# Forget-gate attention and a bilinear feed-forward layer: the two loads of f on two queues, and a new order of all operations

## The chip, the core and the metric

One NeuronCore of one Trainium2 chip. Five engines work beside each other, each through its own list of instructions in order: TensorE (PE; its weight loads are shown as PEld), VectorE (DVE), ScalarE (ACT), GpSimd (POOL) and SyncE (SP), which here only issues DMA transfers. An engine waits on semaphores for the work of others. Matrix products go to PSUM, of which the kernel uses eight banks: four single ones ("ff") and two pairs ("sc"). The metric is the time of one execution on the device in microseconds (us).

## What is computed

Attention with a forget gate over 8 batches of 8 heads, 576 positions of 64 channels, then a feed-forward layer without activation over the 4608 tokens of 512 channels:

```python
scores = scale * np.matmul(q, k.transpose(0, 1, 3, 2))
cum = np.cumsum(np.log(np.clip(f, 0.0001, 1.0)), axis=-1)
decay = cum[:, :, :, None] - cum[:, :, None, :]
scores = np.where(causal, -1000000000.0, scores + decay)
attn = softmax(scores)                       # max taken off, sum + 1e-9
x = (attn @ v).transpose(0, 2, 1, 3).reshape(B * S, H * D)
out = (x @ w_a) * (x @ w_b) @ w_out          # 512 -> 1536 -> 512
```

## The kernel before

The kernel first makes a list of 2353 operations (class `Op`): each has an engine (or a choice of engines), a planned duration, what it depends on, which buffers it takes, and a function that issues its instructions. Then it issues them in an order that is written out in the file as numbers (`ORDER`, at the end), with one letter for each operation that has a choice of engine (`CHOICE`: D, A, P for DVE, ACT, POOL, S for SP), and with the buffer that each taker of a ring gets (`SLOTS`). `laid_out` (L1330) reads the two lists. The order is not one in time: it fixes the list of every engine, and semaphores do the rest.

**Attention** runs in 32 units t = 4 b + pair, each of a batch b and a pair of heads. The 576 queries of a unit are five blocks of rows: 0 to 3 with 128 rows each, 4 with the last 64 rows of both heads. Per unit: PE makes the scores (`sc`, operations qk), DVE takes the maximum of each row (in batch 0) or adds the decay and takes the maximum in one instruction (L674, later batches), ACT exponentiates with the sum (L705; result in PA for blocks 0 to 2 and PB for 3 and 4), DVE inverts the sums (L715), and the probabilities are normalised (`do_norm`, L717: operations norm, mostly on POOL, L726). They are transposed, by PE in batch 0 and partly in batch 1 (`pe_tr`, L742, `psP`: operations ptr, and pev for the copy out of PSUM), else by a DMA transpose on SP's queue (`do_tr`, L736, operations tr, results PTA and PTB). PE multiplies them with v (`do_pv`, L755, pv; pvx for a whole unit), and a copy puts the result into xT (ev). "norm3.0" is a normalisation of unit 3, block 0; there are two, one for each head.

**Loads.** q and k of batch 0 are loaded by POOL's queue with conversion. From batch 1 on SP loads a half batch of q or k at a time as float32 (576 KB, L339), and POOL scales or casts it (`cast_qk`, operations ca1q0 and so on, L291 and L293); PE transposes it into qT or kT (pt, `psT`). The float32 buffers are a ring of three. v of batches 0 and 1 is loaded by POOL (lds, L305), weights too (ldwa, ldwb, ldwo, L510); POOL is then occupied with issuing.

**f** (8 x 8 x 576 values) goes into one tile of the S ring, two halves on partitions 0 to 31 and 64 to 95 (`f_load`, L211, issued at L213). DVE clips it (L225), ACT takes the logarithm (L260), DVE runs the prefix sum (`scan`, L228), all of it in two pieces of columns, 0 to 255 and 256 to 575. A 16-bit high part (L264) and low part (`low_part`, L233, four operations) go into crow, from which PE adds the decay to the scores of batch 0. SP stores the sums to DRAM (`cum_store`, L238), and later units load them spread over all partitions.

**Feed-forward.** xT is cut into groups of 256, 256, 256, 384, six times 512, and 384 tokens. For every group PE makes x w_a (psa) and x w_b (psb), each in groups of matmuls into one PSUM bank (`ff_mm`), ACT copies psa (acopy, L289), DVE multiplies it with psb (mul, L1073), PE multiplies with w_out (pso) and ACT or DVE copies the result for the store. The first psa needs the rows 0 to 255 of all four units of batch 0: blocks 0 and 1, that is norm, ptr, pev, pv and ev of units 0 to 3. Every product is issued as two halves of 64 output partitions (`mm_halves`, L74), which run side by side.

Before that PE has too little to do; 24 operations `wake` (L79, four matmuls on the identity each) stand between its other work.

Of the kernel before, what the change touches and what calls it, by code (L numbers as in the profile page):

```python
# [25 lines left out]
def kernel(  # L26
# [78 lines left out]
    def paddings():  # L105
# [36 lines left out]
        PA:03212103210321032103210321032103;PB:01010101010101010101010101010101;S:010110010110100110101010100101  # L142
        00101010101011101010101011010100111011011001001011010111010101010101011100001010101010;a16:0210210210210
        21021021021021012012012012012012102101201201201201201210212101201012012010210210121010210210210210210;bc
        :0210210210210210210210210210;ff:03120313021332010331032103231232320013100203120103212130213021021032031
        20312031202120131102310230210312031023102310230123123102132013201201320123103213012312301231213201321023
        01321020132013203120312013201321321302103210321032132132013023120320310132103210321032131203121023102130
        23023203103130213213201320132103210312012312031231030123021021021301302130123013013211302012012013202301
        230210231023120312301321302301023021021021021023120121023013203203203203201;ht:0dcba981234567d0bc9a18325
        4760dbc9a187352460da9bc13786524d0a931bc578624d019a35bc7286d9401ab35c728496db01a5c73248906;n16:0101001010  # L150
        10101101010101010010;n32:0210212010210102012012012102101201210120202102;nv:01010101;osb:0101010100101010
        00101101010011010101;qd:010101010101010101010101;sc:0101010101010101101010101010010101010000011010010101
        0100110101101010110101010100010110101001011010101001010100110101010010101010;st:054321054320154320154320
        15432015
# [86 lines left out]
    o_f = [Op(None, {"SP": 0.5, "ACT": 0.5}, lambda e, half=half: f_load(e, half), prio=-310, land=0.3, name=f"ldf{half}") for half in range(2)]  # L241
# [967 lines left out]
    for n in cuts:  # L1209
# [3 lines left out]
        0 1 52 46 29 30 2 62 5 3 53 47 58 4 31-33 37 38 34 39 35 40 42 41 43 267 279 262 6 7 48 54 8 9  # L1213
# [3 lines left out]
        66 141 339 340 21-23 264 67 220 226 94 179 76 96 232 133 221 227-229 271 222 231 180 233 234 84  # L1217
# [4 lines left out]
        200 163 196 1710 292 281 293 1712 201 295 309 310 302 296 303 283 297 1713 164 1715 1714 311-313  # L1222
# [17 lines left out]
        567 698 520 560 534 533 559 540 615 659 630 624 623 625 631 1791 1792 633 632 1790 440-442 569  # L1240
        704 626 491 576 705 492 598 627 599 583 706 619 1793-1798 707 653 714 600 601 1799 614 493 586
# [4 lines left out]
        655 592 564 671 1823 606 721 726 657 664 730 737 738 1824 683 678 732 731 1825 1826 739-741 1827  # L1246
# [3 lines left out]
        811 649 753 1849 776 1850 608 1851 1852 748 750 777 1853-1855 727 901 1857 781 754 788 783 782  # L1250
# [9 lines left out]
        1903 886 880 935 948 942 949 918 919 930 1904 1905 888 950 889 1906-1908 953 1910 1909 1912 809  # L1260
        1013 1101 936 1911 954 1914 891 890 1913 920 810 1915 955 972 929 970 887 881 975 867 927 1019
        882 976 937 922 875 978 1916 1920 1918 990 983 1917 985 1921 892 984 977 991 993 893 894 1919
        956 974 1922 1925 992 979 986 958-960 1923 943 997 980 994 1107 961 998 962 973 1108 1109 1926
# [110 lines left out]
```

## Time and profile before

| | us |
|---|---|
| median of three runs | 402.25 |
| these runs | 400.26, 402.25, 405.24 |
| the profiled execution | 400.81 |
| its span, first to last instruction | 399.0 |
| start of the first psa, from the span's start | 40.70 |
| ACT busy | 288.1 |
| DVE busy | 295.6 |
| POOL busy | 259.1 |

The granted clock of PE has a mean of 0.996 over the span. All times of the profile count from the span's start. A line of the timeline gives start, duration, engine, source line, operation, output and inputs with their shapes, how many instructions are merged, and in brackets how long the engine stood idle before and what ended that. A line of the chain of waits gives start, duration and what the end of the program waited for at that moment; "issue" is time without a wait that the profile shows.

### The profile page before, as it was taken

The page shows a single profiled execution, that of the slowest core. Times are in us where ns is not written, and L with a number is a line of the kernel's source. Part 1 is how long each engine was busy: PE and PEld are TensorE (multiplying, and loading weights), DVE is VectorE, ACT ScalarE, POOL GpSimd, SP SyncE. Part 2 cuts the span into 40 slices and gives each one's busy share as a digit, 9 for nine tenths or more (in the row PEclk, how much of TensorE's full clock was granted, in tenths as well). Part 3 has the DMA queues.
Part 4 walks back from the last instruction along what each step waited for, and adds up shares of the span by engine and source line. Part 5 has one row for each costly group of instructions (what it writes and reads, how often), then busy time and mean ns, then how long its engine had stood idle before and what let it go on. Part 6 is the DMA issues. An engine that isn't in the chain of part 4 may idle for free.

```text
span 399.0 us, 14669 instructions
## 1 busy us (share of the span) xinstructions
PE 388.0 (97%) x5768; PEld 241.0 (60%) x5768; DVE 295.6 (74%) x973; ACT 288.1 (72%) x799; POOL 259.1 (65%) x468
## 2 busy tenths in 40 slices
PE   6988999999999999999999999999999999999997
PEld 3545886978857655555555655555555556555675
DVE  6866899999989979886978887889888780243241
ACT  4996998899889887878887887867887772332131
POOL 8398866698798789596879789687847871000000
PEclk9998999999999999999999999999999999999999
DMA  8899999999999999999999999999997677200102
GB/s 125 232 199 150 128 146 169 285 187 290 248 261 254 246 250 246 226 279 275 266 200 277 258 246 208 254 260 324 183 173 201 113 125 143 86 2 27 54 28 81
DMA packets 147365, 76.87 MB, mean 193 GB/s; under 512 B 124384, under 2 KB 128352, under 8 KB 147296
## 3 DMA queue, kind: packets, MB, share of 16 engines
q1 hardware_dynamic: 132816, 68.65, 75.3%
q0 software_dynamic: 14256, 7.08, 14.6%
q8 instruction: 45, 0.74, 0.7%
q10 hardware_dynamic: 224, 0.21, 0.2%
q14 instruction: 24, 0.20, 0.1%
HBM read 52.05 MB, written 9.58 MB: 154 GB/s over the span
## 4 chain that ended last, share of the span: by engine, by line
PE 88%; DMA 4%; POOL 3%; issue 1%; DVE 1%; ACT 1%; SPq 1%; ACTq 0%; POOLq 0%; DVEq 0%
PE psb L74 23%; PE psa L74 23%; PE pso L74 23%; PE sc L551 4%; PE pvx L769 3%; PE sc L539 2%; PE psT L359 2%; PE psP L74 2%; DMA q<-in_q_dram 2%; PE sc L74 2%; DMA PTA<-PA 2%; POOL PA L726 1%; PE pv L769 1%; PE pvx L784 1%; DMA cum_f<-in_f_dram 1%
## 5 line engine op out<-in xcount | busy, mean ns | idle before, releaser
L674 DVE CUSTOM_DVE_ANT_0 S<-sc,spread 64x576 f32<-64x576 f32 (+4 forms) x232 | 125.2, 561 | 9.9 <-ACT PA L705 2.8
L74 PE MATMUL psa<-xT,wa 128*64 128x512 f16 (+2 forms) x1056 | 113.1, 341 | 0.1
L74 PE MATMUL psb<-xT,wb 128*64 128x512 f16 (+2 forms) x1056 | 113.0, 341 | 0.0
L1073 DVE TENSOR_TENSOR ht<-psb,a 128x512 f16<-128x512 f32 (+1 forms) x114 | 74.1, 659 | 39.3 <-PE psb L74 29.4
L74 PE MATMUL pso<-wout,ht 128*64 128x512 f16 x840 | 101.7, 380 | 0.0
L289 ACT CAST a<-psa 128x512 f16<-128x512 f32 (+1 forms) x114 | 63.2, 557 | 53.1 <-PE psa L74 45.6
L726 POOL TENSOR_SCALAR PA<-PA,st 128x256 f16<-128x256 f16 (+2 forms) x182 | 85.8, 484 | 12.7 <-DVE st L715 11.5
L705 ACT ACTIVATE PA<-S,st 128x256 f16<-128x256 f32 (+2 forms) x168 | 84.1, 503 | 8.2 <-DVE st L674 8.1
L726 POOL TENSOR_SCALAR PB<-PB,st 128x512 f16<-128x512 f16 (+1 forms) x91 | 64.2, 713 | 24.6 <-DVE st L713 11.3
L74 PEld LDWEIGHTS <-wa 128*64 128x64 f16 x1056 | 57.8, 110 | 34.1 <-issue 3.4
L74 PEld LDWEIGHTS <-wb 128*64 128x64 f16 x1056 | 57.6, 110 | 31.5 <-issue 1.3
L74 PEld LDWEIGHTS <-ht 128*64 128x64 f16 x912 | 48.0, 110 | 34.5 <-issue 0.9
L705 ACT ACTIVATE PB<-S,st 128x512 f16<-128x512 f32 x56 | 40.2, 719 | 4.5 <-DVE st L674 4.3
L705 ACT ACTIVATION_READ_ACCUMULATOR PA<-S,st 128x1 f32 x168 | 32.0, 190 | 0.0
L293 DVE COPY osb<-pso 128x512 f32<-128x512 f32 x18 | 12.4, 688 | 19.7 <-DMA out_dram<-osb 10.1
L631 POOL TENSOR_SCALAR_AFFINE_SELECT spread<-spread 128x768 f32<-128x768 f32 x24 | 20.9, 872 | 7.7 <-DMA spread<-cum_d 7.6
L769 PEld LDWEIGHTS <-nv 128*64 128x64 f16 x640 | 21.7, 110 | 6.6 <-DMA PTA<-PA 0.8
L701 ACT ACTIVATE PB<-S,st 128x576 f16<-128x576 f32 x28 | 21.7, 774 | 4.6 <-POOL spread L631 1.2
L674 DVE CUSTOM_DVE_ANT_1 S<-sc,spread 128x256 f32<-128x256 f32 x48 | 19.5, 419 | 6.1 <-ACT xT L289 1.9
L674 DVE DVE_READ_ACCUMULATOR2_ANT st<- 128x1 f32 (+1 forms) x280 | 23.0, 82 | 0.0
L715 DVE RECIPROCAL st<-st 128x2 f32<-128x2 f32 x128 | 18.2, 156 | 6.3 <-ACT PB L705 3.7
L551 PE MATMUL sc<-kT,qT 64*128 64x512 f16 (+4 forms) x144 | 21.3, 333 | 0.8 <-ACT PA L705 0.4
(106 smaller groups left out, 490.3 us busy)
## 6 DMA issues: line engine op xcount, KB each, us to landing
spread<-cum_d SPq DMA_DIRECT2D x24, 576.0 KB, 6.2
out_dram<-osb SPq DMA_DIRECT2D x35, 256.0 KB, 3.1
q<-in_q_dram SPq DMA_DIRECT2D x14, 576.0 KB, 5.6
k<-in_k_dram SPq DMA_DIRECT2D x14, 576.0 KB, 5.4
v<-in_v_dram SPq DMA_DIRECT2D x24, 256.0 KB, 5.9
wout<-in_moe_w_out_dram POOLq DMA_DIRECT2D x3, 512.0 KB, 5.8
nv<-in_v_dram POOLq DMA_DIRECT2D x8, 128.0 KB, 4.2
wa<-in_moe_w_a_dram POOLq DMA_DIRECT2D x2, 512.0 KB, 6.5
```

Of the source, the lines that this page charges most:

```text
L74: nc.tensor.matmul(out=out[r], lhsT=lhsT[:, r], rhs=rhs, **kw)
L289: nc.scalar.copy(out=out_, in_=in_)
L293: VEC[e].tensor_copy(out=out_, in_=in_)
L551: nc.tensor.matmul(out=dst, lhsT=lhsT, rhs=rhs, start=start, stop=stop, skip_group_check=True)
L631: nc.gpsimd.affine_select(out=c[:, :, 0:SM].rearrange("p h (j k) -> p h j k", k=128), in_=c[:, :, SM:2 * SM].rearrange("p h (j k) -> p h j ...
L674: nc.vector.tensor_tensor_reduce(out=o, in0=x, in1=y, scale=-1.0, scalar=3e38, op0=ADD, op1=MIN, accum_out=m)
L701: nc.scalar.activation(out=p_blocks(t, 4), in_=T[("s" if direct else "z", t, 4)], func=EXP, bias=st[:, 8:9], scale=sign, accum_out=st[:, 1 ...
L705: nc.scalar.activation(out=p_blocks(t, i)[:, :, h, :], in_=(T[("s", t, i)][:, h, :] if direct else T[("z", t, i)][:, h * n:h * n + n]).rea ...
L715: nc.vector.reciprocal(out=st[:, 20 + 2 * i:22 + 2 * i], in_=st[:, 10 + 2 * i:12 + 2 * i])
L726: VEC[e].tensor_scalar(out=p, in0=p, scalar1=st[:, c:c + 1], scalar2=1.0, op0=MUL, op1=MUL)
L769: nc.tensor.matmul(out=o[HP[h], 128 * i:128 * i + 128], lhsT=vt[:, j, pr + NP * h, :], rhs=pt[:, base_blk[i] + 2 * block_at(t, i, j) + h, ...
L1073: nc.vector.tensor_tensor(out=ht[:, 0:n_], in0=T.pop(("psb", t0, fbs))[:, 0:n_], in1=T.pop(("a16", t0, fbs))[:, 0:n_], op=MUL)
```

## The change

The two loads of f had a choice of SP or ACT, and both letters were A. Now the first half is issued by SP and the second by ACT, without a choice, so `CHOICE` has 231 letters instead of 233. `ORDER`, `CHOICE` and `SLOTS` are replaced as a whole. The operations themselves, their instructions and the sizes of all rings are the same. The core of the diff:

```diff
--- before.py
+++ after.py
@@ -139,19 +139,19 @@
     SLOTS = """
-        PA:03212103210321032103210321032103;PB:01010101010101010101010101010101;S:010110010110100110101010100101
...
+        PA:03210213021302130213021302130213;PB:01101010101010101010101010101010;S:010110100110100110101011001101
...
@@ -238,7 +238,7 @@
-    o_f = [Op(None, {"SP": 0.5, "ACT": 0.5}, lambda e, half=half: f_load(e, half), prio=-310, land=0.3, name=f"ldf{half}") for half in range(2)]
+    o_f = [Op(("SP", "ACT")[half], 0.5, lambda e, half=half: f_load(("SP", "ACT")[half], half), prio=-310, land=0.3, name=f"ldf{half}") for half in range(2)]
     for o in o_f:
         o.issue, o.units = 0.5, 32
@@ -1210,121 +1210,121 @@
     ORDER = """
-        0 1 52 46 29 30 2 62 5 3 53 47 58 4 31-33 37 38 34 39 35 40 42 41 43 267 279 262 6 7 48 54 8 9
-        56 50 44 36 10 63 82 55 11 49 83 45 287 71 268 73 85 91 65 64 57 86 92 87 93 288 12 59 51 97 127
-        98 99 60 13 14 172 15 88 61 130 136 289 175 181 131 138 137 132 16 128 17 290 269 176 182 183
-        177 173 142 184 139 291 178 187 143 144 270 189 188 186 280 500 274 18 217 19 20 218 185 263 90
-        66 141 339 340 21-23 264 67 220 226 94 179 76 96 232 133 221 227-229 271 222 231 180 233 234 84
-        24 145 190 235 223 103 135 140 191 236 225 72 224 134 75 203 204 109 237 341 89 147 192 95 265
...
+        0 1 29 30 46 2 52 62 5 3 31 37 32 38 33-36 39 40 42 41 53 47 58 4 43 267 262 279 6-9 54 48 10 56
+        50 44 11 63 82 55 83 12 13 49 45 85 91 97 57 65 64 86 92 87 93 51 94 14 127 59 130 136 88 99 98
+        95 96 287 66 61 67 268 90 263 60 288 172 15 131 16 138 132 137 128 269 17 175 181 176 177 183
+        182 289 290 142 291 173 187 184 100 144 143 18 217 19 270 189 188 20 218 274 500 178 220 226 221
+        228 227 222 89 102 72 339 145 139 232 340 223 185 141 71 73 180 179 101 21 22 113 271 341 133
+        135 264 233 234 140 84 265 229 103 190 114 186 225 266 74 134 104 105 23 121 203 24 158 109 204
+        110 25 342 211 159 235 115 116 106 236 230 343 212 129 76 224 275 192 237 231 107 75 191 280 391
...
     CHOICE = """
-        AADPDDADAAADAAAPAPPPPAPAAADPAAPPPPPPDDDDPPPAPAPPPDAAAPPPPPPPPPADAAADADADDADDPPAPPPPAPDDADAAP
-        PAPAPPADAAPPPPPPAPADAAAPPPPPPPPPAADADDDAADDDADAADAAAADAADAADDADADDAAAADADAADADDADADAADDDAAAD
-        AAADAADAADADAADDAADAAADDAAADADAADDDADDAAADADDDDAD
+        DDDDADADADAAPPAPPPAPPAADAPPPPPPAPADDDDPPPAPPPPPDDDDPAAPAPPPADDDADAADAAAADDPPPAPAPPPADDAAPPAP
+        PAPAADADAAAPPPPPPDDDAPPPPPPPPPAADAAAAADADDAAAAADADDADADDAADDDAADAADDDADADDAAAADADDAADAAAADDA
+        AAAADADAAAADAAAADAAADAAAAADADAAAADAADDAADDDAAAD
```

The lists that the new numbers make, written with the names of the operations (a nameless one has a word in brackets). SP up to the fifth load of q or k:

```
before  (cum_store) ld1q0 ld1q1 ld1k0 ld2q0 ld1k1
after   ldf0 (cum_store) ld1q0 ld1k0 ld1q1 ld1k1 ld2q0
```

POOL up to the last norm3.0, without the loads of batch 0 and the constants ahead of it:

```
before  flo1 (paddings) bc04 ldwa ca1q0 ldwb ca1q1 norm2.0 ca1k0 norm0.1
        lds0v0 norm1.0 bc05 lds0v1 norm2.1 ldwa norm0.0 norm3.0 norm2.1
        norm2.2 norm3.2 norm3.1 ldwa norm3.1 norm1.1 ldwa norm3.2 norm1.2
        norm0.3 bc06 norm3.0
after   (paddings) norm0.0 bc04 lds0v0 lds0v1 ca1q0 norm0.1 ca1k0 norm0.1
        norm0.2 ldwa bc05 norm2.0 norm1.0 ldwa ldwb norm2.1 norm2.1 norm0.2
        norm1.1 norm1.0 ldwb norm1.1 ldwa norm3.1 ca1k1 norm2.2 norm3.2 norm3.0
```

(bc04 and its like clear a strip of the spread buffer; flo is a low part.) PE up to the first psa, from the first transpose of probabilities:

```
before  ptr2A0 wake ptr0A0 ptr1A0 wake bm5 ptr2A1 qk1.2 ptr3A0 pv2 wake pv0
        wake pv3 bm6 ptr0B pv1 ptr3A1 qk2.2 ptr0A1 ptr0B psa
after   ptr0A0 pt1k0 qk0.2 wake pv0 ptr2A0 wake ptr1A0 wake bm5 pv2 ptr0A1
        qk1.2 wake ptr3A0 wake pv1 ptr2A1 wake ptr3A1 bm6 pv3 qk2.2 psa
```

DVE's list at the start, from f's arrival: before (clip, scan, clip, high part, scan, low part, high part, low, low, maximum of block 1 of unit 0), after (clip, clip, scan, high part, low, low, scan, high part, low, low, maximum). The copies out of PSUM, the norms and the copies of results are dealt out anew between DVE, ACT and POOL in all batches; the counts by engine are DVE 679 to 677 operations, ACT 512 to 517, POOL 426 to 422, SP 160 to 161.

More of the change, by code (lines that the diff above doesn't have):

```diff
@@ L141 @@
     SLOTS = """
-        PA:03212103210321032103210321032103;PB:01010101010101010101010101010101;S:010110010110100110101010100101
[L143 to L151, printed above, removed]
@@ L152 @@
-        00101101010011010101;qd:010101010101010101010101;sc:0101010101010101101010101010010101010000011010010101
-        0100110101101010110101010100010110101001011010101001010100110101010010101010;st:054321054320154320154320
-        15432015
+        PA:03210213021302130213021302130213;PB:01101010101010101010101010101010;S:010110100110100110101011001101
+        01010101001010101010101010010011010100101001000100010011011010011100111011010101110101;a16:0210210210210
+        21021021021021021021201201210210210210201201201012012021021021020120120201010201210201201201201201021;bc
@@ new lines @@
+        :0210210210210210210210210210;ff:03120312032100023120310323231232301230103010103203013120312031203120312
+        03123012310120213203203013203210312013201320130123021312312031232013012013023103210131310321320312031023
+        10210321032130230231023102312302130213021321023023012032032031310210210312310231302132013203210310231023
+        20120210102120321312012013203103021301321301302102302310230132031203120132013012012021023101301321032132
+        030231031031032031230123201230312312312312312312302311021021302301231231230;ht:0dcba981234567d0bc9a18234
@@ L155 @@
+        5670dbc9a182543d670cb9a1428653d70cb2a9154863d7bac025914863dcb7a9205148dc36a9b72051483cdb6;n16:0110100101
+        10001010010101010101;n32:0210201201201201020101212110210220201212202101;nv:01010101;osb:0101010101001010
+        10101010010100110101;qd:010101010101010101010101;sc:0101010101010101010101011010010101100010101011001001
+        0101101010101011010101010101010100101011101100101010110101100101100100101010;st:054321503421503421503421
+        50342150
     """
@@ L1263 @@
-        956 974 1922 1925 992 979 986 958-960 1923 943 997 980 994 1107 961 998 962 973 1108 1109 1926
[40 rows of a table removed]
-        2125 1582 1519 2126 1584 1521 1589 1564 1556 1565-1567 1583 1585 1590 1596 1520 1597 1568 2127
[6 rows of a table removed]
-        1648 2159 1593 1681 1594 1630 1688 2164-2166 1691 2163 2168-2171 2167 1692 2172 1527 2138 1528
[4 rows of a table removed]
-        1704 1574 2200 1662 2195 2196 2201 1705 1706 2205 2207-2209 2212 2214 2216 2213 2210 2217 2218
-        2220 2219 2222 2221 2215 2224 2226 2225 2227 2223 2228 2230 2232 2233 2229 2234 2236 2238 2237
@@ new lines @@
+        630 1792-1794 618 493 491 1795 492 494 631 702 707 653 654 703 697 1797 569 704 626 623 632 619
[4 rows of a table added]
+        1827 1829-1831 709 719 723 767 671 681 591 729 628 724 647 636 682 655 648 641 1828 666 1832 686
[15 rows of a table added]
+        1920 1914-1918 929 918 766 1919 951 970 975 1014 852 851 896 895 1871 919 1921 958 920 959 955
[17 rows of a table added]
+        1265 2001 1203 1147 1260 2002 1175 1310-1312 1100 1226 1204 1196 1233 1205 2005 2006 1197 1206
+        2008 2009 1207-1210 1168 1327 1167 2010 1220 2012 1243 2011 1126 1227 1212 2013 1238 1996 2014
@@ new lines @@
+        1244 1198 1217 2015 1189 2016 2017 1239 1245 1321 1184 1228 1234 2018 1219 1262 1240 1266 1248
+        1249 2020-2022 1250 1251 1268 1267 2019 2024 1264 2025 1252 1287 1288 1269 1289 2026 2028 2029
[6 rows of a table added]
+        2061 1362 1364 1258 2059 1363 1376 1380 1354 1365 1366 1381-1383 1394 1384 1395 1387 2062 1317
[3 rows of a table added]
+        2077 2074 2081 1428 1431 1432 2079 1439-1441 1434 1433 1461 2082-2084 1423 1422 1464 2086 1367
[5 rows of a table added]
+        1413 1515 1575 1517 2110 1538 1454 1540 2109 1539 1494 1546 1495-1498 2112 2113 1552 2114 1554
[3 rows of a table added]
@@ new lines @@
+        1584 1597 1598 1591 1599 1592 2129-2131 1564 1562 1565 1585 1566 1580 2134-2136 1459 1619 2128
[10 rows of a table added]
+        2193 1617 1701 1702 1574 2194 2195 1618 2197 2198 1703 1660 1704 2199 2202-2204 1705 1661 2207
+        2208 2205 2196 2206 2200 1662 1706 2209 2212 2214 2216 2213 2210 2215 2218 2220 2221 2217 2211
+        2201 2222 2219 2224 2226 2225 2223 2227 2228 2230 2232 2233 2229 2231 2260 2234-2242 2244 2245
[4 rows of a table added]
+        2322 2321 2323-2327 2329-2335 2338-2340 2343-2345 2336 2341 2342 2337 2346-2352
```

13 lines of the change are left out of this document (removed), and 174 rows, old and new, of the table ORDER.

## The prediction

> **What bounds the kernel now.** I read the first line of the page, then a table of stretches that I cut at the first matmul of the feed-forward part (40.70 us) and at the end of the last matmul (396.1 us), with a fourth row for a place where the clock falls.
>
> ```profile
> span 399.0 us, 14669 instructions
> ```
>
> ```profile
> 0.00:40.70 40.70, 33.28 (x571) 19.71 (x573) 29.20 (x72) 30.77 (x88) 30.87 (x65) 0.96 0.94 177
> 40.70:396.10 355.40, 354.71 (x5204) 221.30 (x5198) 266.07 (x902) 257.31 (x712) 228.27 (x404) 1.00 0.91 195
> 396.10:399.00 2.90, 0.02 (x2) 0.00 (x0) 0.29 (x1) 0.00 (x0) 0.00 (x0) 1.00 0.28 87
> 31.90:35.30 3.40, 3.34 (x33) 1.76 (x31) 2.09 (x4) 0.80 (x1) 3.37 (x8) 0.50 1.00 145
> ```
>
> Behind the window stand its length, the busy time of PE, PEld, DVE, ACT and POOL, the granted clock, the DMA share and GB/s. From 40.70 us on PE idles 355.40 - 354.71 = 0.69 us in all. A busy PE need not be at its peak, so I looked at groups of its matmuls in the chain of waits:
>
> ```profile
> 183.29 0.98 PE psa L74 x8
> 184.55 0.86 PE psb L74 x8
> ```
>
> Eight feed-forward matmuls over 512 columns run as 4 pairs, the two halves side by side, and take 0.86 us: 0.215 us for a pair. Nearly all such groups in the chain show 0.86 or 0.87, so this is the rate of the whole middle. Its matmuls are the same before and after, and no order makes them fewer. The last 2.90 us (copy and store of the last piece) keep their order too. What can be won lies in the first 40.70 us, where PE runs fill-in matmuls on `wake` and waits. There the chain begins so:
>
> ```profile
> 0.81 1.30 ACTq L213
> 2.10 0.03 issue
> 2.13 3.59 DMA cum_f<-in_f_dram
> ...
> 12.26 7.75 DMA q<-in_q_dram
> ```
>
> After f come the scan on DVE, the store of the sums and, behind it on SP's queue, the first two loads of batch 1; the second of these lands at 20.01 us, and then POOL carries the chain until PE takes over.
>
> **Part 1: f on two queues.** ScalarE's first issue holds back the second from 0.81 to 2.13 us, 1.32 us; the second half lands at 2.13 + 3.59 = 5.72 us. With both issued at about 0.8 us (SP has nothing to do then) f is there at 4.4 us.
>
> ```profile
> 5.83 0.29 DVE L225 TENSOR_SCALAR cum_f<-cum_f 96x256 f32<-96x256 f32 x1 [0.86 <-DMA cum_f<-in_f_dram]
> 6.60 0.69 DVE L228 TENSOR_TENSOR_SCAN cum_f<-cum_f,cum_l 96x256 f32<-96x256 f16 x1 [0.48 <-ACT cum_l L260]
> 7.20 0.30 DVE L225 TENSOR_SCALAR cum_f<-cum_f 96x320 f32<-96x320 f32 x1
> 7.42 0.38 DVE L264 CAST crow<-cum_f 96x256 f16<-96x256 f32 x1
> 8.04 1.33 DVE L228 TENSOR_TENSOR_SCAN cum_f<-cum_f,cum_l 96x320 f32<-96x320 f16 x1 [0.24 <-ACT cum_l L260]
> 9.41 0.42 DVE L233 TENSOR_TENSOR crow<-cum_f,crow 32x256 f16<-32x256 f32 x1
> ```
>
> DVE waited 0.86 us for f; until 5.83 - 0.86 = 4.97 us it makes other constants. So of the 1.32 us 0.86 arrive, and the first scan ends at 6.60 + 0.69 - 0.86 = 6.43 us. The new order then puts the cast and both low parts of these columns (one was POOL's) ahead of the second scan: 0.38 + 2 x 0.42 = 1.22 us. The second scan ends at 6.43 + 1.22 + 1.33 = 8.98 us, before at 8.04 + 1.33 = 9.37. Store and loads behind it on SP's queue go out 0.4 us sooner. A rule of the Trainium skill speaks against this part (DMA: Bandwidth & Descriptors, "Issuing engines are not separate DMA queues"): issuing on several engines saves only the issue time, usually little beside the transfer. The trace agrees, 1.32 beside 3.59 us; with nothing saved, my sum would come out 0.4 us higher.
>
> **Part 2: POOL's order ahead of the first feed-forward matmul.** This is the main term. First POOL's groups from 15 to 36 us (busy, mean ns of one, idle before), then two moments of its timeline.
>
> ```profile
> L726 POOL TENSOR_SCALAR PA<-PA,st 128x384 f16<-128x384 f16 x6 | 3.5, 583 | 0.1
> L726 POOL TENSOR_SCALAR PA<-PA,st 128x256 f16<-128x256 f16 x6 | 2.8, 477 | 0.1
> L291 POOL TENSOR_SCALAR q<-q 128x1152 f16<-128x1152 f32 x2 | 2.3, 1153 | 6.2 <-DMA q<-in_q_dram 6.2
> L293 POOL CAST k<-k 128x1152 f16<-128x1152 f32 x2 | 2.3, 1142 | 0.0
> L510 POOL DMA_DIRECT2D wa<-in_moe_w_a_dram x3 | 1.9, 650 | 0.0
> L305 POOL DMA_DIRECT2D nv<-in_v_dram x2 | 1.9, 936 | 0.0
> L726 POOL TENSOR_SCALAR PA<-PA,st 128x128 f16<-128x128 f16 x5 | 1.8, 372 | 0.1
> ```
>
> ```profile
> 20.19 1.15 POOL L291 TENSOR_SCALAR q<-q 128x1152 f16<-128x1152 f32 x1 [1.57 <-DMA q<-in_q_dram]
> ...
> 33.65 0.93 POOL L726 TENSOR_SCALAR PA<-PA,st 128x128 f16<-128x128 f16 x2
> ```
>
> POOL waits 6.2 us for two loads of q, the second until 20.19 us, and then hardly at all up to norm3.0, the last normalisation that the first feed-forward matmul needs: the first of the two at 33.65 us, done at 33.65 + 0.37 = 34.02. The new order uses the waits: both nv issues (1.9 us) and the first norms go ahead of the first q, and the cast of the second q goes far behind. On SP's queue k takes the second place from that q, so now POOL waits for k: a load of the same size in the same place, 20.19 - 0.4 = 19.8 us. From that cast to the last norm3.0 the new list holds 2 casts of 1.14, 4 norms of 128 columns (0.372), 6 of 256 (0.477), 4 of 384 (0.583) and 5 weight issues (0.650): 2.28 + 1.49 + 2.86 + 2.33 + 3.25 = 12.2 us. norm3.0 ends at 32.0 instead of 34.02 us.
>
> The bounds: the least is no wait for k at all; POOL is through with the first q and one norm at 20.19 - 1.57 - 0.4 = 18.2 at the latest, and norm3.0 ends at 30.4. The most is that all of it is lost to later landings (the weight issues stand closer together now) but for f's 0.4: 33.6. I take 32.0, since the row for the second load is that of the same queue place.
>
> ScalarE's list up to its last needed step loses 11 entries (five norms, four copies out of PSUM, a copy for `spread`, an f load) and gains five; DVE's grows from 54 to 57. In the first stretch DVE was busy 29.20 and ACT 30.77 of 40.70 us; I price both at nothing beside POOL. If that cover is missing, one PSUM copy more on DVE costs 0.54 us (row below).
>
> **Part 3: from the last norm to the first psa.** Before, 40.70 - 34.02 = 6.7 us, much of it a backlog from the 3.40 us at a clock of 0.50 (31.9 to 35.3 us).
>
> ```profile
> 37.94 0.45 PE psP L74 x16
> 38.39 0.17 PE pv L769 x6
> 38.55 0.34 PE psP L74 x12
> 38.89 1.24 PE sc L551 x18
> 40.13 0.74 PE psP L74 x22
> 40.86 0.21 PE psa L74 x3
> ```
>
> ```profile
> 38.59 0.42 DVE L293 CAST xT<-pv 128x256 f16<-128x256 f32 x1 [0.24 <-PE pv L769]
> 38.93 0.15 DVE L713 RECIPROCAL st<-st 128x1 f32<-128x1 f32 x1
> 39.00 0.54 DVE L293 COPY xT<-psP 128x768 f16<-128x768 f16 x1
> ```
>
> In the new list the path is: transpose 0.34, a wake of two pairs 0.43, pv 0.17, DVE's cast 0.42 and copy 0.54, pv 0.17, score group 1.24: 3.31 us, and 0.4 for the hand-overs (my allowance; one of 0.24 stands in the row). First psa at 32.0 + 3.7 = 35.7 us, 5.0 sooner. This takes the full clock. The Trainium skill (TensorE: Matmul & The Clock Gate, "What's actually happening") has the clock halve after an idle window of about 3.4 us and come back after a busy one; the trace's 3.40 us at 0.50 agree in length. Should the half clock fall on this path, its PE share (0.34 + 0.43 + 0.17 + 0.17 + 1.24 = 2.35 us) doubles.
>
> **Part 4: behind psa.** Two groups of `psP` transposes now stand behind the first psa, one of 16 matmuls (0.45) and one of 10 (0.28 at the same rate): +0.7 us. In PE's list behind it the changes between matmuls on 64 and on 128 rows go from 112 to 108. The group at 183.29 us stands behind such a change and took 0.98, the one at 184.55 us 0.86: 4 x 0.12 = -0.5 us. Copies and norms that change between ACT, DVE and POOL cost nothing as long as PE's list is full: these engines were busy 257, 266 and 228 of 355 us.
>
> **The sum.** -5.0 + 0.7 - 0.5 = -4.8 us. Against the profiled execution (400.8 us, of which the span is 399.0) that is 396.0. The median of the three runs is 402.25 (400.26 to 405.24); there it is 397.5. By the bounds of Part 2: 30.4 + 3.7 = 34.1, so -6.6 + 0.2 = -6.4, 395.9; or 33.6 + 6.7 = 40.3, so -0.4 + 0.2 = -0.2, 402.0.
>
> **The rivals.** *The start doesn't move.* The loads land late, or PE meets another late engine, and only f's 0.4 us stays: 402.0. For it: the DMA share of the first stretch is 0.94 already, and f's path has other work behind it. Against it: POOL's list is shorter whatever lands. Chance 0.20.
>
> *More than forecast.* k is there when POOL wants it (395.9), the 0.69 us of idle time go too, and the runs lie where the lowest run before lay, 2 us below the middle: 393. Chance 0.12.
>
> *Slower: PE's list in order waits at pv for transposes by DMA*, with ready feed-forward work behind it.
>
> ```profile
> L769 PE MATMUL pvx<-PTA,nv 128*64 128x128 f16 x288 | 14.8, 219 | 0.3 <-DMA PTA<-PA 0.3
> ```
>
> Before, all 24 of these groups (12 matmuls each) waited 0.3 us together. If the new order brings the norms and so the transposes late by a little each time, 24 waits of 0.7 us are 16.8: 397.5 + 16.8 = 414. It decides from 12.8 us on, 0.53 a group. Against it: counted in PE work on the two lists, a transpose stands in the middle 4.7 us ahead of its pv, before 3.8. Chance 0.16.
>
> **How the numbers follow.** Forecast 397.5 us with chance 0.52; rivals 0.20, 0.12, 0.16. 2% (about what a measurement of this kernel can tell from no change) is 394.2 and 410.3 us. The second rival is the share of faster, 0.12, the third that of slower, 0.16; the others give 0.72 within. The range reaches from 393 (second rival) to 406: the first rival's 402.0, the 3 us that the highest run lay above the middle, and 1 us of new waits. Outside are the third rival and a little of the second.
>
> **What would show it.** DVE takes f at about 5.0 us without a wait for DMA; POOL's two waits for loads end at about 16.5 us with q and at 19.8 us with k; norm3.0 at 32.0; first psa at 35.7; behind it under 1.5 us of PE idle. I am wrong if psa starts behind 39 us, or if PE idles over 3 us behind it.

## The result, and the profile after

| | before | after |
|---|---|---|
| median of 13 runs | 401.41 us | 399.45 us |
| lowest and highest | 400.26, 405.24 | 398.51, 400.52 |
| the profiled execution | 400.81 | 399.23 |
| its span | 399.0 | 397.5 |
| start of the first psa | 40.70 | 35.63 |

The ratio of after to before is 0.9933 (95% interval 0.9907 to 0.9959). The start moved by 5.07 us, which is the forecast 5.0; the profiled execution shortened by only 1.6 us and the median by 1.96, where the forecast had 4.8. So the question of this study is where the other 3 us went. Here and below, runs that lie more than 1.5% above the fastest run of their kernel are left out of the ratios.

First the stretches of after, cut as before at the first psa and at the last matmul (behind the window its length, busy PE, PEld, DVE, ACT, POOL, granted clock, DMA share, GB/s):

```profile
0.00:35.63 35.63, 29.97 (x544) 17.69 (x544) 29.59 (x76) 28.37 (x83) 29.51 (x62) 1.00 0.98 187
35.63:394.60 358.97, 356.48 (x5230) 233.22 (x5224) 263.11 (x897) 262.22 (x723) 228.24 (x403) 1.00 0.93 194
```

The second stretch is 358.97 us long, before 355.40: 3.57 us more. Two transpose groups that now stand in it account for 0.73 (0.45 and 0.28, as forecast). PE idles 358.97 - 356.48 = 2.49 us, before 0.69: 1.80 more. The remaining 1.04 us are more busy time for the same matmuls; ends of matmuls are modelled, so short waits can be counted as busy, and I trust the sum of the two more than the parts. The account: -5.07 + 0.73 + 1.80 + 1.04 = -1.50, the difference of the spans.

For what PE waited in after (engine, operation, line, releaser; us in total, times, longest):

```profile
PE pvx L769 <- DMA PTA<-PA: 1.3, 3, 0.8
PE psT L359 <- DMA wout<-in_q_dram: 0.8, 1, 0.8
PE psb L74 <- DMA wb<-in_moe_w_b_dram: 0.5, 1, 0.5
```

Behind psa these are the transposes that pvx needs and a load of weights. The chain of waits of after shows the same two:

```profile
37.07 8.06 DMA wb<-in_moe_w_b_dram
45.13 0.14 issue
45.27 1.06 PE psb L74 x16
...
131.44 6.72 DMA PTA<-PA
```

In before, PE itself carried the chain through the middle (88% of it, now 77%; DMA 4%, now 11%). And SP's and POOL's timelines of after, for the start:

```profile
8.29 0.83 SPq L238 DMA_DIRECT2D cum_d<-cum_f  x2
9.17 0.43 SPq L339 DMA_DIRECT2D q<-in_q_dram  x1
9.65 0.50 SPq L339 DMA_DIRECT2D k<-in_k_dram  x1
10.19 0.48 SPq L339 DMA_DIRECT2D q<-in_q_dram  x1
```

```profile
14.06 0.38 POOL L726 TENSOR_SCALAR PA<-PA,st 128x128 f16<-128x128 f16 x1 [2.92 <-DVE st L715]
...
16.39 1.18 POOL L291 TENSOR_SCALAR q<-q 128x1152 f16<-128x1152 f32 x1
...
17.95 1.14 POOL L293 CAST k<-k 128x1152 f16<-128x1152 f32 x1
...
21.03 0.59 POOL L726 TENSOR_SCALAR PA<-PA,st 128x384 f16<-128x384 f16 x1 [1.48 <-DVE st L715]
...
30.00 1.49 POOL L726 TENSOR_SCALAR PA<-PA,st 128x384 f16<-128x384 f16 x3
...
32.14 0.59 POOL L726 TENSOR_SCALAR PA<-PA,st 128x384 f16<-128x384 f16 x1
```

POOL no longer waits for a load: q and k have no bracket. It waits for DVE's row sums instead, 2.92 and 1.48 us. The three norms merged at 30.00 are norm2.2, norm3.2 and, with 128 columns, the last norm3.0, which ends at 30.00 + 1.49 = 31.49 us. The norm at 32.14 has 384 columns: it is the second norm2.2. The first psa doesn't need its result, but PE's list has the transpose of it (ptr2A1) ahead of psa, so the chain of waits runs through it:

```profile
31.49 0.61 POOL wa L510
...
32.14 0.60 POOL PA L726
...
32.78 0.53 PE psP L74 x12
33.31 0.43 PE wake L74 x4
33.74 0.34 PE psP L74 x12
...
34.46 1.24 PE sc L551 x18
```

### The profile page after: what moved, and what is told of

Its sections match the earlier page's. It is cut to its first block, busy times and chain, and to the rows that moved or that the text cites. A ratio compares the mean times of both kernels' runs of the same rounds, so it can differ in the third digit from the quotient of the medians.

```text
span 397.5 us, 14691 instructions
## 1 busy us (share of the span) xinstructions
PE 386.4 (97%) x5768; PEld 250.9 (63%) x5768; DVE 293.0 (74%) x971; ACT 290.6 (73%) x805; POOL 257.8 (65%) x464
## 4 chain that ended last, share of the span: by engine, by line
PE 77%; DMA 11%; POOL 4%; ACT 3%; issue 2%; DVE 2%; SPq 0%; DVEq 0%; ACTq 0%; POOLq 0%
PE psa L74 21%; PE psb L74 20%; PE pso L74 20%; PE sc L551 4%; DMA PTA<-PA 3%; PE pvx L769 3%; POOL PA L726 2%; DMA PTB<-PB 2%; PE psT L359 2%; DMA wb<-in_moe_w_b_dram 2%; PE sc L539 2%; DMA wout<-in_q_dram 2%; PE sc L74 1%; PE psP L74 1%; DMA k<-in_k_dram 1%
## 5 line engine op out<-in xcount | busy, mean ns | idle before, releaser
L726 POOL TENSOR_SCALAR PA<-PA,st 128x256 f16<-128x256 f16 (+2 forms) x180 | 84.9, 483 | 8.8 <-DVE st L715 5.5
L74 PEld LDWEIGHTS <-wb 128*64 128x64 f16 x1056 | 62.5, 110 | 30.0 <-issue 2.5
L74 PEld LDWEIGHTS <-wa 128*64 128x64 f16 x1056 | 61.7, 110 | 29.3 <-issue 2.2
L726 POOL TENSOR_SCALAR PB<-PB,st 128x512 f16<-128x512 f16 (+1 forms) x90 | 63.4, 711 | 24.3 <-DVE st L715 10.7
L74 PEld LDWEIGHTS <-ht 128*64 128x64 f16 x912 | 49.9, 110 | 33.0 <-issue 1.9
L674 DVE CUSTOM_DVE_ANT_1 S<-sc,spread 128x256 f32<-128x256 f32 x48 | 19.8, 419 | 6.9 <-PE sc L539 2.0
L289 ACT COPY osb<-pso 128x512 f32<-128x512 f32 x24 | 13.8, 580 | 9.1 <-PE pso L74 7.8
```

The costliest lines, as they stand in the source:

```text
L74: nc.tensor.matmul(out=out[r], lhsT=lhsT[:, r], rhs=rhs, **kw)
L289: nc.scalar.copy(out=out_, in_=in_)
L674: nc.vector.tensor_tensor_reduce(out=o, in0=x, in1=y, scale=-1.0, scalar=3e38, op0=ADD, op1=MIN, accum_out=m)
L726: VEC[e].tensor_scalar(out=p, in0=p, scalar1=st[:, c:c + 1], scalar2=1.0, op0=MUL, op1=MUL)
```

## The experiments

Every ratio is to the kernel before, measured in the same set of runs. Its median was 401.41 in the set of after and 402.59, 402.67 and 403.44 in the three sets below, so medians of different sets are not compared.

### Which part moves the start: the split or the order?

**f_only**, the order of before with the loads of f split:

```diff
-    o_f = [Op(None, {"SP": 0.5, "ACT": 0.5}, lambda e, half=half: f_load(e, half), ...
+    o_f = [Op(("SP", "ACT")[half], 0.5, lambda e, half=half: f_load(("SP", "ACT")[half], half), ...
     CHOICE = """
-        AADPDDADAAADAAAPAPPPP
+        DPDDADAAADAAAPAPPPP
```

> The order of before, with f split over SyncE and ScalarE and nothing else changed. Theory A (f's chain drives the start of before): f lands 1.3 us sooner, 0.9 of it reach the two scans, the loads of batch 1 go out 0.9 us sooner and first psa comes at 39.8 instead of 40.7 us; ratio to before 0.998. Rival (the start is bound by POOL and by PE's backlog, f is hidden): first psa stays at 40.5 to 40.9 us, ratio 1.000.

**order_only**, the new order with both halves on ScalarE:

```diff
--- after
+++ order_only
-    o_f = [Op(("SP", "ACT")[half], 0.5, lambda e, half=half: f_load(("SP", "ACT")[half], half), ...
+    o_f = [Op("ACT", 0.5, lambda e, half=half: f_load("ACT", half), ...
```

> The new order, with both loads of f issued by ScalarE. Theory A (the order alone makes the start; in the changed kernel the chain of the first 10 us runs through a load of q and not through f): f lands 1.3 us later, first psa at 35.6 to 36.2 us, ratio to before 0.993 to 0.995, the same as the full change. Rival (the f split is needed for the new order): psa at 36.8 us or later, ratio 0.997 or more.

| | ratio | 95% interval | profile: first psa | from there to the last matmul |
|---|---|---|---|---|
| f_only | 0.9967 | 0.9935 to 0.9999 | 37.10 | 357.90 |
| order_only | 0.9945 | 0.9915 to 0.9975 | 35.27 | 360.03 |
| after (both) | 0.9933 | 0.9907 to 0.9959 | 35.63 | 358.97 |

In these profiles each part alone brings most of the start, and together they bring no more than the order alone. My sum gave the split 0.4 us. SP's and POOL's timelines of f_only show why that was too little; the order of POOL in it is that of before:

```profile
8.15 0.84 SPq L238 DMA_DIRECT2D cum_d<-cum_f  x2
9.03 1.06 SPq L339 DMA_DIRECT2D q<-in_q_dram  x2
10.13 0.47 SPq L339 DMA_DIRECT2D k<-in_k_dram  x1
```

```profile
15.28 1.15 POOL L291 TENSOR_SCALAR q<-q 128x1152 f16<-128x1152 f32 x1 [2.38 <-DMA q<-in_q_dram]
...
17.24 1.15 POOL L291 TENSOR_SCALAR q<-q 128x1152 f16<-128x1152 f32 x1 [0.20 <-DMA q<-in_q_dram]
...
31.43 0.92 POOL L726 TENSOR_SCALAR PA<-PA,st 128x128 f16<-128x128 f16 x2
```

The same lines of SP's timeline of before:

```profile
9.40 0.82 SPq L238 DMA_DIRECT2D cum_d<-cum_f  x2
10.26 2.47 SPq L339 DMA_DIRECT2D q<-in_q_dram  x2
12.77 0.47 SPq L339 DMA_DIRECT2D k<-in_k_dram  x1
```

The store goes out 1.25 us sooner, and the two issues of q behind it take 1.06 instead of 2.47 us. So the second q is taken at 17.24 instead of 20.19, and the last norm3.0, the first of the two norms merged there, ends at 31.43 + 0.37 = 31.80 instead of 34.02: 2.2 us, not 0.4. The other 1.4 of the 3.6 us lie between norm3.0 and psa, 5.30 us here and 6.68 in before: the granted clock up to psa is 1.00 in this profile and 0.96 in that of before, where it was half from 31.9 to 35.3 us. Five of the twelve runs of f_only have such a stretch somewhere, by their mean clock of 0.996, so this part is not the split's in every run. With the new order POOL does not wait for these loads at all, so there the split has nothing left to win. In the profiles psa is even 0.36 us sooner without it, which says little: between kernels with the same lists up to psa it moved by up to 0.95 us (35.63 in after, 34.73 in after_pv_later and 35.68 in after_light, below).

In f_only PE's list is that of before, so each matmul can be set beside its like. This is how far the one ran ahead of the other, worked out from the starts of the matmuls in the two traces:

```
start in before (us)        43.2    55.3    67.4   115.5   175.8   223.9   236.0   393.1
lead of f_only (us)         3.59    3.05    2.68    2.88    2.60    1.66    1.24    1.21
```

The lead doesn't fade, it falls in steps (once, at 79.0 us, it grows by 0.42), and between two steps PE runs at the same speed in both. The larger steps are at psb at 48.5 us (0.54), pso at 62.2 (0.35), pvx at 157.0 (0.28) and 220.4 (0.35), psT at 221.2 (0.58) and psa at 230.9 (0.28). In f_only's waits behind psa, those for loads of wb and wout and for transposes before pvx come to 1.5 us, and those for work of DVE (before psT) and ACT (before psa) to 0.6. In the kernel before the same places hardly waited (0.69 us of idle in all): PE came there up to 3.6 us later.

**new_start_old_rest** and **old_start_new_rest** join the two orders: up to about the first psa the one, behind it the other, each operation with the engine that its own order gives it.

```
new_start_old_rest   ORDER = first 231 operations of after, then the others as in before (f split)
old_start_new_rest   ORDER = first 235 operations of before, then the others as in after (f on ACT)
```

> The new order (and f split) for the 231 operations up to the first psa, the order, engines and buffers of before for all the rest. Theory A (the start gains 5 us and the new order of the rest gives 3 us back in waits of its own): first psa at 35.6 us, PE work behind it as before plus 0.7 us, span 394.7 us, ratio 0.989. Rival B (PE is fed by the attention of the other engines, and an earlier start makes it wait behind psa in any order): first psa at 35.6 us, but 2 to 3 us more idle PE behind it, span 397 to 398 us, ratio 0.993 to 0.996.

> The order of before for the 235 operations up to the first psa, the new order, engines and buffers for all the rest; f on ScalarE alone. Theory A: first psa at 40.7 us, the waits of the new rest stay, 2.5 to 3 us more than before, span 401.5 us, ratio 1.006 to 1.008. Rival B: with 5 us more time for the other engines the waits behind psa vanish, span 398.5 to 399.5 us, ratio 0.998 to 1.001.

new_start_old_rest: 0.9962 (0.9933 to 0.9990), first psa at 37.98, 356.12 us behind it. old_start_new_rest: 1.0087 (1.0048 to 1.0125), 39.85 and 360.35 us, about what theory A had. With the old start, the new rest costs 3.5 us; with the new start the whole execution is no slower with it than with the old rest (0.9933 beside 0.9962, within the intervals). So the gain is the start's. That the new rest fits its own start only is not shown, since both kernels wait at the seam. In new_start_old_rest the old rest has two transposes ptr0B ahead of psa, and the second waits 2.28 us for POOL's normalisation of blocks 3 and 4, until 37.68; so psa came at 37.98 and not at the 35.6 that both theories had. Behind this later psa the old rest needs only 0.7 us more than in before, and 2.85 less than the new rest in after (0.73 of it for the two transposes that stand behind psa there). Where old_start_new_rest waits, from its waits:

```profile
PE psP L74 <- POOL PA L726: 1.5, 1, 1.5
PE psP L74 <- POOL PB L726: 1.2, 1, 1.2
PE pvx L769 <- DMA PTA<-PA: 1.1, 1, 1.1
PE psT L359 <- POOL q L291: 0.6, 1, 0.6
PE pv L769 <- DMA nv<-in_v_dram: 0.5, 1, 0.5
```

The first of these lies in the old start (at 30.28 us, where before waited 1.91), the second at the seam, at 42.51; the other three are behind psa.

### What takes the lead away behind the start?

**after_pv_later** puts 23 of the 24 pvx one feed-forward group later in PE's list, which gives their transposes more time (five of the copies behind them, and two other entries, move a little in the lists of DVE and ACT with it); **after_wb_sooner** puts the last load of wb directly behind the one before it in POOL's list.

```
PE    after            ... qk23.3 psb psa psb pv20 psa psb ...
PE    after_pv_later   ... qk23.3 psb psa psb psa pv20 psb ...
POOL  after            ... ldwb norm1.3 norm1.2 norm1.2 ldwb norm0.4 ...
POOL  after_wb_sooner  ... ldwb ldwb norm1.3 norm1.2 norm1.2 norm0.4 ...
```

> The changed kernel; 23 of the 24 pvx groups of units 8 to 31 stand one feed-forward group (0.65 to 0.87 us of PE) later in PE's list. Wait theory (part of what the start gained is lost at pv, waiting for transposes by DMA): PE's idle time behind psa falls from 2.5 to about 1 us, span 396 to 396.5 us, ratio to before 0.989 to 0.991. Rival (what PE is given later it waits for later, the buffers of the transposes come free later and the next transposes with them): idle stays at 2 us or more, ratio 0.993 or more.

> The changed kernel; POOL issues the last load of w_b directly behind the one before it, 1.7 us sooner, ahead of three norms. Wait theory: the wait of the psb at 44 us for w_b (0.5 us idle) goes, first psa unmoved at 35.6 us, span 397.0 us, ratio to before 0.992. Rival: the load comes no sooner beside the others, or the norms that stand behind it make PE wait as long: wait of 0.4 us or more at that place, span 397.5 us.

after_pv_later: 1.0065 (1.0030 to 1.0101), slower than after by some 5 us. after_wb_sooner: 0.9960 (0.9927 to 0.9992), not better than after. In its profile the wait for wb is gone, but pvx waits 1.8 us for transposes, and PE idles 4.10 us behind psa (2.49 in after). Behind psa after_pv_later waited so:

```profile
PE psT L359 <- ACT osb L289: 1.2, 2, 1.0
PE psb L74 <- ACT a L289: 0.7, 1, 0.7
PE sc L74 <- ACT xT L289: 0.7, 1, 0.7
PE sc L539 <- ACT qT L289: 0.7, 2, 0.4
PE sc L539 <- ACT xT L289: 0.5, 1, 0.5
PE pvx L769 <- DMA PTA<-PA: 0.5, 1, 0.5
```

The wait for transposes fell from 1.3 to 0.5 us, as intended, and the operations behind a later pvx then met copies on ACT: counted from the starts of PE's matmuls, those other than pvx stood for some 10 us behind psa, in after for some 2.4. A wait that a profile names is not a wait that can be taken away by itself: the list is tight on several engines at once.

**before_light** and **after_light** cut the transfers: of nearly every store only 128 of the 512 columns are left, so most of the output is not written. In the kernel before and in after alike, the DMA engines show a mean share over 1 from the first psa up to 240 us. These are two stretches of before, then of after:

```profile
80.00:120.00 40.00, 39.90 (x758) 30.05 (x755) 36.90 (x131) 36.20 (x102) 35.57 (x62) 1.00 1.17 246
160.00:240.00 80.00, 80.00 (x1066) 43.76 (x1064) 65.97 (x237) 64.75 (x186) 62.34 (x114) 1.00 1.09 253
```

```profile
80.00:120.00 40.00, 40.00 (x729) 29.76 (x726) 36.83 (x133) 34.62 (x98) 32.59 (x59) 1.00 1.12 252
160.00:240.00 80.00, 79.16 (x1100) 45.80 (x1098) 65.81 (x230) 62.84 (x181) 62.67 (x113) 1.00 1.11 248
```

If the transfers are a second bound close behind PE, fewer bytes should help after more than before.

```diff
-        nc.sync.dma_start(out=out[r0:r0 + 128, :], in_=T.pop(("osb", t0, tb)))
+        nc.sync.dma_start(out=out[r0:r0 + 128, 0:128], in_=T.pop(("osb", t0, tb))[:, 0:128])
```

> The kernel before, with each full store of the result cut to its first 128 of 512 columns (35 stores of 64 KB instead of 256 KB; 6.9 of 76.9 MB of transfers are left out, and so are 384 columns of most of the output). Theory of the full queues: what the earlier start wins is given back because transfers behind the first feed-forward matmul land too late for PE (the DMA share there is 0.91 to 0.93). In the kernel before PE stood only some 1.3 us in its list behind that matmul, so with fewer bytes little can come: ratio 0.994 to 0.999. Rival, the hand-overs between engines hold PE and not the transfers: 0.999 to 1.002, and the same step for this kernel and the next.

> The kernel after with the same cut of the stores (384 columns of most of the output are left out). Theory of the full queues: PE stood 4.1 us behind its first feed-forward matmul in the profile of after, 3 us of it at products that wait for transposes or weights that come by DMA; at least half of this goes: ratio to the kernel before 0.983 to 0.988 (397.8 to 395.8), and the distance from the kernel before with the same cut grows from 2 us to 3.5 to 5. Rival, the hand-overs between engines: 0.991 to 0.996 as without the cut, and the distance stays at 2 us.

before_light: 0.9943 (0.9910 to 0.9975). after_light: 0.9893 (0.9839 to 0.9947, six runs). The distance between the two is 0.0050, about 2 us, and no more than the 0.0067 without the cut: before_light lies where the theory of the full queues had it, after_light between the two expectations. The growth to 3.5 us or more did not show, and the interval is too wide to exclude it. The profiled executions look more like the theory: behind psa before_light needs 355.59 us (before 355.40), after_light 356.72 (after 358.97). But before_light's shows nothing of the 0.57% that its ratio has.

```profile
40.81:396.40 355.59, 354.73 (x5204) 221.12 (x5199) 265.80 (x902) 257.39 (x712) 227.34 (x404) 1.00 0.88 176
```

```profile
35.68:392.40 356.72, 355.73 (x5230) 231.60 (x5224) 262.89 (x896) 262.25 (x723) 227.09 (x403) 1.00 0.88 177
```

Set matmul beside matmul, after_light gains on after at psb at 45.3 us (0.63), at pvx at 120.8, 138.3 and 173.0 (0.26, 0.37, 0.29) and at psb at 150.1 (0.25), nearly all at work that had waited for transfers. But at 45.3 us no result has been stored yet, so the 0.63 there is the difference of two executions and not the cut's, and the other gains rest on one execution of each kernel too. The cut was also a weak one: the share behind psa fell only from 0.93 (before 0.91) to 0.88. That PE's waits at these places end with a transfer is what the traces show; that it is the load of the transfers, and not the moment at which they are issued, is not shown.

### The clock and the spare matmuls

The profiled before had a stretch of 3.4 us at half clock ahead of psa, the profiled after none. Each run lists its mean clock, and one such stretch lowers it by about 0.0043. Of 86 runs of before, in the three sets of experiments, those without one have a mean of 401.16 us (21 runs), with one 402.61 (38), with two 403.84 (25), with three 405.8 (2): some 1.3 us for each. None of the 13 runs of after has one. The distance of the means in the set of after is 402.15 - 399.46 = 2.69 us; if 401.16 holds in that set too, about 1 us of it goes with the clock (402.15 - 401.16). Whether the clock is its cause was to be tried.

**before_filled** has more spare matmuls where before waits ahead of psa, to hold the clock up; **after_unfilled** and **before_unfilled** leave the later 12 of the 24 wake operations empty, which lets PE go idle.

```diff
--- before_filled, in pe_tr behind the allocation of psP
+        for _ in range({(1, "A0"): 30, (2, "A0"): 14}.get((t, part), 0)):
+            mm_halves(p[:, 0, :], ident16, ident16, is_transpose=True, start=True, stop=True, skip_group_check=True)
--- after_unfilled, before_unfilled
-        o = Op("PE", 0.427, lambda _: wake(2), ...
+        o = Op("PE", 0.427, lambda _, n=n: wake(2 if n < 12 else 0), ...
```

> The order of before; ahead of the transposes of the probabilities of units 1 and 2, block 0 and 1, PE makes 30 and 14 pairs of spare 128-column transposes of the identity (2.3 us) in the time in which it stood idle for POOL's norms. Clock theory: the stretch of 3.4 us at clock 0.50 behind this idle time goes; mean clock 1.0 in most runs (before: about 1 run in 3), first psa at 37.5 to 38.5 instead of 40.7 us, and each such stretch is worth 1.3 us of the whole, so ratio to before 0.996 to 0.998. Rival (the half clock only lies in time that PE loses anyway): psa sooner, but ratio 1.000.

> The changed kernel, in which the last 12 of the 24 wakes make no matmul. Clock theory: PE has too little to do between 18 and 34 us, the clock falls to 0.50 in most runs, first psa comes 1 to 4 us later in those, and a run costs 1.3 us for each stretch of 3.4 us: ratio to before 0.996 to 1.003. Rival (the new order's gain is that of POOL's list alone, which does not run on PE's clock): first psa at 35 to 36 us and ratio 0.993 as with all wakes.

> The kernel before, in which only the first 12 of the 24 wake operations issue matmuls (the others issue nothing). Theory: the spare matmuls from about 17 us on stand in PE's list ahead of work that the start needs, and hold it back by more than the full clock is worth: first feed-forward matmul about 1 us sooner (39.7), granted clock 0.991 or below from two or more stretches at half clock ahead of it, ratio 0.994 to 0.998. Rival, the half clock falls on the work between the last normalisation and that matmul: it starts no sooner than 40.7 and the ratio is 1.000 to 1.006.

> The kernel after with only the first 12 wake operations filled, once more, since its first result (0.9861, 0.9817 to 0.9905) rests on six runs. If the gain over the kernel after is real, the ratio is 0.984 to 0.990 again; if it was the luck of few runs, 0.991 to 0.996, the kernel after's own.

| | ratio | 95% interval | mean clock of its runs | first psa |
|---|---|---|---|---|
| before_filled | 1.0043 | 1.0005 to 1.0081 | 0.998 to 1.000 in 9 of 12 | 39.45 |
| before_unfilled | 1.0014 | 0.9978 to 1.0049 | 0.979 to 0.992 | 40.22 |
| after_unfilled | 0.9861 | 0.9817 to 0.9905 | 0.990 to 1.000 | 34.57 |
| after_unfilled_again | 0.9885 | 0.9845 to 0.9925 | 0.991 to 1.000 | 34.73 |

The price of 1.3 us a stretch does not carry over. before_filled has hardly any and starts 1.25 us sooner, and is slower, where the theory of the clock had 0.996 to 0.998. before_unfilled has two to five such stretches in every run and is as fast as before. after_unfilled has them in nine of its twelve runs, with a mean of 398.4 us, and none in three, with 399.2. More likely the clock and the time have one cause: in runs in which PE waits longer, it also falls to half clock. That is argued from these kernels and not shown. Behind psa before_filled needs 360.45 us, and PE idles 4.45 of them, 3.8 more than in before:

```profile
39.45:399.90 360.45, 356.00 (x5204) 223.23 (x5200) 266.12 (x903) 257.14 (x712) 227.48 (x404) 1.00 0.93 194
```

Of before_unfilled the theory had the clock right, but psa came only 0.48 us sooner instead of 1, and the ratio is that of its rival. The granted clock up to psa is 0.83 in its profile, and 0.76 from the last norm3.0 (34.09) to psa, where PE is nearly always busy; so there the half clock does fall on work that the start needs:

```profile
0.00:40.22 40.22, 29.70 (x522) 18.64 (x524) 28.95 (x72) 30.66 (x88) 30.82 (x64) 0.83 0.95 176
```

In the new order, with the same edit, the first psa comes at 34.57 and 34.73 instead of 35.63, with a clock of 1.00 up to there in both profiles. That is not shown to be the edit's: after_pv_later has all spare matmuls and the lists of after up to psa, and its psa came at 34.73 too. What can be seen is the way from the end of the norm2.2 in the chain above to psa: it took 2.90 us in after and in after_pv_later, and 2.47 and 2.46 without the spare matmuls. The 0.43 us between them are as long as the wake that stands there in the chain. For after_unfilled both theories had expected less than came.

after_unfilled is the fastest kernel of the study. Against before it is shown twice, by six runs each; against after it has not been measured in one set. The two ratios lie below after's 0.9933, the first with an interval that ends just below after's (0.9905 and 0.9907), the second with one that overlaps it.

## Why the prediction was right, and where it was off

The forecast 397.5 us lies 1.95 us below the result, inside the range, and the change stayed within 2%, as forecast. Its base was high by 0.84 us: the median of 13 runs is 401.41, that of the first three was 402.25. Against its own base the gain came out at 1.96 us instead of 4.75. Step by step:

- **Part 1, f: mis-sized.** The clip of f started at 4.54 us (with a wait of 0.51, since DVE was done with the constants at 4.03, where the forecast had 4.97), and the second scan ended at 8.27, forecast 8.98: 0.37 us because it started sooner, 0.34 because it took 0.99 instead of 1.33 us. The bigger error is "loads behind it on SP's queue go out 0.4 us sooner": the third left at 10.19, before at 12.77, because the issues themselves became shorter (below). In the order of before, the split is worth 2.2 us at norm3.0, not 0.4. The rule of the Trainium skill that I set beside it (DMA: Bandwidth & Descriptors, "Issuing engines are not separate DMA queues") agrees for the transfer of f: DVE took it 1.29 us sooner, beside the 1.32 us of issue time that I had read. It has no price for what a sooner start decides further down the queue.
- **Part 2, POOL: nearly the right end, wrong wait.** The wait for k until 19.8 us wasn't there, which was my lower bound: its cast began at 17.95. Behind it a wait of 1.48 us for DVE's row sums took most of that back (another, of 2.92, lies ahead of the first q). That is the row which I had priced at nothing ("I price both at nothing beside POOL"). From the cast of k to the end of norm3.0 it took 13.54 us, 12.06 without the wait, forecast 12.2. norm3.0 ended at 31.49, forecast 32.0.
- **Part 3, to psa: too short, and by another path.** 35.63 - 31.49 = 4.14 us, forecast 3.7. My path ran from norm3.0 over its transposes and DVE's copy to psa. The chain above runs over an issue of a weight and the norm2.2 at 32.14, whose transpose stands in PE's list ahead of psa, and from there PE works without a pause. That norm3.0 is the last norm before psa is right for the data and wrong for PE's list. The errors of parts 2 and 3, 0.5 and 0.4 us, cancel, and psa at 35.63 beside 35.7 owes its precision to that luck. The full clock, which the step needed, was there.
- **Part 4, behind psa: the step that failed.** The 0.73 us of moved transposes came. The 0.5 us for fewer mode changes cannot be seen in it: the stretch got 2.84 us longer beside the 0.73, not 0.5 shorter. The sentence that failed is "Copies and norms that change between ACT, DVE and POOL cost nothing as long as PE's list is full". PE's list was in order but not ready: PE came 5 us sooner, but the last wb landed at 45.13 us, only some 2.5 sooner than in before (41.86 + 5.7 = 47.6), and pvx waited 1.3 us for transposes. PE idled 2.49 us, above the 1.5 that I had set as a sign and below the 3 that would have been wrong.
- **The rivals.** "The start doesn't move" fell with psa. The mechanism of the slow rival, pvx waiting for transposes by DMA, appeared: 1.3 us in three waits, far from the 12.8 from which it decides. "More than forecast" did not come, though its premise (k there in time) did.

What stays open is why no more than 1.6 us (in the profile) to 2.7 us (in the means) of the 5 are kept. Shown, on the old order, is that a lead is lost in steps of 0.3 to 0.6 us; on the new one, that PE waits for transfers at the places named; and that curing one place by itself (a later pvx, an earlier load) brought nothing or made it worse.

## What to carry to other kernels

A gain at the start of a long pipeline is worth its size only as far as every other engine and every transfer follow; before adding it to the sum, go through the first places behind it where the leading engine met its data without waiting, and ask how much sooner those data come. Where two edits shorten the same wait (here the earlier loads, and an order that has other work in their place), each alone shows most of the gain at the start (3.6 and 5.4 us here, 5.1 together), and they must not be added. Spare matmuls that are to hold the clock up can have a price of their own: test the kernel with half of them gone. And before giving an edit a microsecond of one profile, see how far the same point moves between executions of unchanged lists: here it was 0.95 us.

## What the runs showed of the hardware that was not expected

**The issue of a load took 0.43 or 1.95 us.** It is the same instruction on SP's queue, 576 KB of q. In the chain of waits of before its first issue starts at 10.26 us and takes 1.95; in after it starts at 9.17 and takes 0.43.

```profile
10.26 1.95 SPq L339
```

In order_only the first two, at 9.59 and 10.16, take 0.53 each, and the third, at 10.73, takes 1.18:

```profile
9.59 0.53 SPq L339 DMA_DIRECT2D q<-in_q_dram  x1
10.16 0.53 SPq L339 DMA_DIRECT2D k<-in_k_dram  x1
10.73 1.18 SPq L339 DMA_DIRECT2D q<-in_q_dram  x1
```

In f_only a pair of them, from 9.03 us on, took 1.06; in the traces of five kernels with the old start and f on ScalarE alone the pair, from 10.24 to 10.49 us on, took 1.73 to 2.57. So the early pair went through, and the later ones were held. The time alone does not decide it: in after_unfilled_again the issue of k at 10.08 took 1.30 us, in after_wb_sooner that of q at 10.42 took 0.47. What holds an issue, no run here tells. It is how, in f_only, 1.25 us at the store became 2.6 us at the third load (10.13 instead of 12.77).

**A scan of the same shape took 1.33 or 0.88 us.** The second prefix sum (96x320) took 1.33 us in before at 8.04 us, 0.99 in after at 7.28 and 0.88 in f_only at 7.24:

```profile
7.24 0.88 DVE L228 TENSOR_TENSOR_SCAN cum_f<-cum_f,cum_l 96x320 f32<-96x320 f16 x1 [0.24 <-ACT cum_l L260]
```

In order_only it took 0.88 us at 7.83. In all five traces in which it took 1.25 to 1.34 us (before, before_light, before_filled, before_unfilled, old_start_new_rest), POOL made its low part (L233, some 0.67 us, which reads the same tile) and four clears and copies in that time; in the nine in which it took 0.88 or 0.99, POOL ran other instructions (L97, L102). That the low part is what slows it is not tested.
